# A planner's durations, landings and fillers: new numbers for the order of a DeltaNet and SwiGLU kernel

## The chip, the cores and the metric

The kernel runs on one core of a Trainium2 chip. A core has TensorE (PE) for matrix products, which go to eight PSUM banks; VectorE (DVE), ScalarE (ACT) and GpSimd (POOL) for elementwise work; and SyncE (SP), which here only issues DMAs. Each engine runs its own instructions in the order in which the program lists them, and waits for the others through semaphores. The metric is the device time of one execution in microseconds. A measured time of this kernel can be told from no change if it differs by over 0.2%.

## The reference

Two blocks follow each other. The first is a delta-rule recurrence, for 4 batches of 8 heads over 768 steps with a head size of 48:

```python
k_n = k / (np.linalg.norm(k, axis=-1, keepdims=True) + 1e-06)
for t in range(S):
    kt, vt, bt = (k_n[:, :, t], v[:, :, t], beta[:, :, t, None])
    y[:, :, t] = np.einsum('bhd,bhde->bhe', q[:, :, t], state)
    v_old = np.einsum('bhde,bhd->bhe', state, kt)
    state = state + bt[:, :, :, None] * np.einsum('bhd,bhe->bhde', kt, vt - v_old)
```

Its output, as 3072 tokens of 384 features, goes through an RMS norm with a gain and a gated FFN of width 1536:

```python
rms = np.sqrt(np.mean(x * x, axis=-1, keepdims=True) + 1e-06)
xn = x / rms * rms_g
g = xn @ w_gate
silu = g * (1.0 / (1.0 + np.exp(-g)))
return (silu * (xn @ w_val) @ w_out).astype(np.float32)
```

The FFN's weights arrive as 64-bit floats.

## The kernel before, in words

**Chunks.** The 768 steps are cut into 12 chunks of 64. Within a chunk the recurrence is solved as a triangular system; from chunk to chunk a state is carried. For each chunk there is a preparation (norms of k, a transpose of k (`turn`, TensorE line 565), the products of k with itself (`scores`, line 588), a solve of small triangular blocks on VectorE, and several round trips through DRAM that put the blocks into other layouts), a part with q (`qpart`), the recurrence proper (`recur`) and the FFN.

**Chunks 0 and 1** are prepared by `prep16`, which solves blocks of 16 steps. The blocks are copied out by ScalarE (L756), written to DRAM (`dm<-at`) and read back as `dg` (`mt<-dm` for chunk 0, `kk<-dm` and `wsum<-dm` for chunk 1). A TensorE step called `coupling` (L778) makes the parts that couple the blocks. In `recur`, a first product (`first_rows`, L1055, for chunk 0; `mr`, L1041, for chunk 1) is followed by three rounds of `couple` (L1067), each with differences on VectorE (`change`, L1112) between; chunk 0 does this for two halves of its heads in turn. Then come the products with q (`pu`, L1077), the new state (`ku`, L1146), the norm, and a transpose (L1217) whose copies (L1221) are the FFN's input `xf`, or `xp1` for chunk 1. The FFN of chunks 0 and 1 (`ffn_plain`, L1284 and L1266) works with the plain weights. Later chunks use `prep`, with blocks of 32, and a form of the FFN with fewer products (`ffn` and `down`, L1377 and L1434) on sums of weights which VectorE makes once (`factors`, L1342; `out_factors`, L1413).

**Weights.** `weights` brings the 64-bit weights in 24 tiles of 768 KB through three raw buffers. ScalarE takes the upper words (L506), VectorE makes a shift, a mask and a product (L494, L497, L502), and then two 32-bit parts are added. For the first `NPE` = 4 tiles TensorE does that addition, as two products with the identity into PSUM (L518, L519), which ScalarE copies out (L523). For the others VectorE adds (L526).

**The planner.** Nothing of the order is written by hand. Every step is given to a planner with its engine, an assumed duration, a priority or due time, what it reads and writes, and the PSUM banks that it takes. `forward` simulates the engines: at each point it takes the step that can start first, and among equals the one with the lower key. `backward` makes new keys from the result, and 60 rounds of this, some with small random shakes, are tried; the order of the round with the earliest simulated end is written out. The assumed numbers thus do not delay anything by themselves on the chip: they set the order in which each engine is given its instructions, and the order of the DMAs on SP's queue.

Three things of it matter here. A DMA has an earliest simulated start (`after`), a transfer time (`work`) and a latency until others may use its data (0.7, for weight tiles 0.7 + 2.0). A TensorE step's duration in the simulation is a number in the code: 0.5 for `coupling`, 0.49 for each half of `first_rows` and `couple`. And up to a simulated time of 70 us, the planned gaps between TensorE's steps are filled with products of the identity with itself (`filler`, L1538), which write a bank that nobody reads. `fillers` decides how many: it takes a planned gap from `a` to `b`, and adds products of four, two or one times 128 columns, until less than 0.3 is left; a gap of over 1.5 is first lengthened by 0.8. Fillers are in TensorE's queue like any other instruction, and a step that comes after them starts after them.

Of the kernel before, what the change touches and what calls it, by code (L numbers as in the profile page):

```python
# [19 lines left out]
W = 32  # L20
L = 16
# [7 lines left out]
STICK = 1.0  # L29
SHAKE = 0.12  # L30


# [20 lines left out]
def fillers(a, b):  # L53

    if a == 0.0:
        return [4, 4, 1]
    n, t = [], a
    while t < b - 0.3:
        n.append(4 if b - t > 1.5 else 2 if b - t > 0.9 else 1)
        t += 0.22 * n[-1] + 0.02  # L60
    return n


class Plan:
# [154 lines left out]
    def run(self, free, filler=None, until=0.0):  # L219
# [19 lines left out]
        for op, s in best[1]:  # L239
# [4 lines left out]
            if filler and op.eng == "PE":  # L244
                if s < until:
                    filler(fillers(pe, s + (0.8 if s - pe > 1.5 and pe else 0.0)))
                pe = s + op.dur
# [9 lines left out]
def kernel(  # L257
# [54 lines left out]

    WLAT = 2.0
    NPE, NRAW, NCV = 4, 3, 2
    WCOL = 768
    CV2 = 90.0
    NK, NKQ = 3, 2
# [69 lines left out]
    def dma(dst, src, prio, r=(), w=(), work=0.3, dur=0.5, eng="SP", after=0.0):  # L387
        queue = nc.scalar if eng == "ACT" else nc.sync
        op = P.add(eng, dur, lambda: queue.dma_start(out=dst, in_=src), prio, r, w, lat=0.7)  # L389
        op.dma, op.work, op.ready, op.port = True, work, after, False  # L390

    PERIOD = 51.0
# [53 lines left out]
    def zeros_out():  # L446
        dma(dm.rearrange("g x s t -> (g x s t)").rearrange("(p n) -> p n", n=1024), mt[0].rearrange("p x t -> p (x t)"),
            5, r=mtkeys(0), w=[("dm", z) for z in range(4)], work=2.0, dur=0.6, after=16.8)

    def load_small():  # L450
        for i in range(8):
            src = beta.rearrange("b (y g) (c i t) -> i g (b y) c t", i=2, g=2, t=W)[i // 2 % 2, i % 2]
            dma(beta_b[16 * i : 16 * i + 16], src, 0.5, w=[("beta", i)], work=0.2, after=0)
        for z in range(2):
            rows = slice(64 * z, 64 * z + 64)
            P.add("ACT", 0.25, lambda rows=rows, z=z: nc.scalar.copy(b16[rows], beta_b[rows, 0:2, L * z : L * z + L]), 3, r=[("beta", i) for i in range(4 * z, 4 * z + 4)], w=[("b16", z)])
        dma(g_sb, moe_rms_g.rearrange("(t p) -> p t", p=128), 1, w=["g"], after=33)

# [5 lines left out]
    def weights():  # L464
# [14 lines left out]
        for n, (dst, src, keys) in enumerate(todo):  # L479
# [3 lines left out]
            rdst = raw[i].rearrange("p (a c) -> p a c", a=parts)  # L483
            dma(rdst, src, (0.1 if n == 0 else 3 + 2 * n), w=[("raw", i)], dur=0.7, work=3.06, after=(6.0, 29.5, 32.8, 33.1, 41.3, 40.8, 44)[n] if n < 7 else 48)

            P.ops[-1].lat = 0.7 + WLAT
            low, high = (raw[i].bitcast(U32)[:, w_ : w_ + 2 * WCOL - 1 : 2] for w_ in range(2))
# [45 lines left out]
    def load(c, what):  # L533
        t0 = c * C
        pk, pq, pv = ((-5, 1, 12), (5, 29, 36))[c] if c < 2 else (due(c, 150), due(c, 99), due(c, 70))
        if "q" in what and c > 1:
            for d, eh, g, th in itertools.product(range(2), repeat=4):
                e0, e1 = 32 * eh, min(D, 32 * eh + 32)
                src = q.rearrange("b (yh a) t e -> a t (b yh) e", a=4)[2 * d + g, t0 + 32 * th : t0 + 32 * th + 32, :, e0:e1]
                r0 = 64 * d + 32 * eh  # L540
                dma(q2t[r0 : r0 + 32, :, g, th, 0 : e1 - e0], src, pq, w=[q2k[8 * d + 4 * eh + 2 * g + th]], work=0.2, after=40.1)
        for key, t, src, pr in (("k2", k2[c % NK], k, pk), ("q2", q2, q, pq)):
            for g in range(2):
# [3 lines left out]
                s = src.rearrange("b (y g) t e -> g t (b y) e", g=2)[g, t0 : t0 + C]  # L547
                dma(dst, s, pr, w=[(key, c % NK, g)] if key == "k2" else q2k[8 * g : 8 * g + 8], dur=0.7, work=1.02, eng="ACT" if c == 0 and g and key == "k2" else "SP", after=((0.0, 18.2, 0.0), (2.9, 46, 0.0))[c]["kqv".index(key[0])] if c < 2 else 40.1)
        if "v" in what and c == 0:
            for g in range(2):  # L550
                s = v.rearrange("b (y g) t e -> g t (b y) e", g=2)[g, 0:C]
                dma(vt[64 * g : 64 * g + 64], s, pv, w=[("v", g)], dur=0.7, work=1.02, after=10.1)
        elif "v" in what:
            for bb in range(2):
                s = v[2 * bb : 2 * bb + 2, :, t0 : t0 + C, :].rearrange("p h t e -> t (p h) e")
                dma(vt[64 * bb : 64 * bb + 64], s, pv, w=[("v", bb)], dur=0.85, work=1.02, after=44.0 if c < 2 else 62.1)

# [78 lines left out]
    def prep16(c):  # L636
# [57 lines left out]
        for r0, b0, n in place:  # L694
            dma(a16[c][r0 : r0 + W], dk.rearrange("g x j t -> (g x) j t")[:, b0 : b0 + L, b0 : b0 + L], pd, r=[("dfull", c, g) for g in range(2)], w=[("ab", c, n)], dur=0.55, work=0.5, after=25 if c else 0.0)
        ab = [("ab", c, n) for n in range(4)]
# [73 lines left out]
        for h in range(2):  # L770
# [10 lines left out]
            P.rows = 64  # L781
            P.add("PE", 0.5, coupling, pi, r=dgk + ["under"] + (kkall if c else []), w=[ps] + ek, ps=ps, size=64)
            P.rows = 128
# [188 lines left out]
    def recur(c):  # L972
# [141 lines left out]
        for h in halves:  # L1114
# [4 lines left out]
            else:  # L1119
                P.add("PE", 0.49, lambda h=h: first_rows(h), pr, r=[("dg", 0, g) for g in range(2)] + mtkeys(0) + vk, w=gu + uk(h) + zk(h), ps=gu, size=64)  # L1120
            P.rows = 128
# [4 lines left out]
            for n in range(3):  # L1126
                P.rows = 64
                P.add("PE", 0.49 * len(h), lambda h=h, t=zb if n else u_: couple(h, t), pr, r=ek + (zk(h) if n else uk(h)), w=gu, size=64 * len(h))
                P.rows = 128
# [444 lines left out]
```

## Time and profile before

| | |
|---|---|
| median of 3 runs | 708.71 us (708.32 to 708.85) |
| the profiled execution | 709.8 us |
| its span, first to last instruction | 708.1 us |
| TensorE busy | 697.1 us (98%) |
| VectorE busy | 538.9 us (76%) |
| ScalarE busy | 305.4 us (43%) |
| fillers (L1538) busy | 43.0 us, all before 72 us |
| granted TensorE clock, mean | 0.999 |

Times in the profile are microseconds from the start of the span. "L778" is line 778 of the kernel. The chain of waits is followed back from the last instruction; each of its rows has a start, a length and what ran. An engine's timeline has start, length, engine, line, operation and tiles, and in brackets how long the engine was idle before and what it waited for. An fp32 product is listed as two instructions, so "x64" is 32 products; a transpose is one. A TensorE that runs fillers counts as busy.

### The profile page before, as it was taken

Reading aid. Unit: us, or ns where it says so; the run is one execution under the profiler, and the core shown is the slowest. Engines: PE = TensorE matmul, PEld = TensorE weight load, DVE = VectorE, ACT = ScalarE, POOL = GpSimd, SP = SyncE. Lnnn points to the kernel's source line nnn. Section 1 sums busy time; section 2 is a strip of 40 time slices with the busy share of each in tenths; the row PEclk is TensorE's granted clock in tenths of the full one; section 3 lists DMA queues with packets and bytes.
Section 4 is the critical chain, followed back from the end, with each engine's and each line's share of the span. In section 5 each row is a group of like instructions: output and inputs, shape, how many; then the busy total and the mean of one; then the engine's idle time right before and its main releaser. Section 6 shows DMA issues by size and latency. Waiting matters only on the chain.

```text
span 708.1 us, 23662 instructions
## 1 busy us (share of the span) xinstructions
PE 697.1 (98%) x10178; PEld 635.7 (90%) x10178; DVE 538.9 (76%) x1129; ACT 305.4 (43%) x739; POOL 141.6 (20%) x143
## 2 busy tenths in 40 slices
PE   9999999999989999999999999999999999999997
PEld 5677887778869999999999989999999999999997
DVE  3553799999999978959849949959869838957473
ACT  5244544343314635544535445445446345236241
POOL 6002012103141332132132132133132103000000
PEclk9999999999999999999999999999999999999999
DMA  7569683664620252353252352343342160030000
GB/s 155 116 183 216 174 215 84 167 119 77 108 53 14 45 104 45 64 94 57 45 96 51 50 90 49 56 82 56 58 88 44 27 116 7 14 65 2 23 1 24
DMA packets 236585, 55.49 MB, mean 78 GB/s; under 512 B 225856, under 2 KB 228928, under 8 KB 236480
## 3 DMA queue, kind: packets, MB, share of 16 engines
q1 hardware_dynamic: 232304, 53.19, 38.6%
q8 instruction: 80, 1.31, 0.8%
q10 hardware_dynamic: 4176, 0.79, 0.5%
q14 instruction: 25, 0.20, 0.1%
HBM read 40.83 MB, written 13.11 MB: 76 GB/s over the span
## 4 chain that ended last, share of the span: by engine, by line
PE 88%; DVE 4%; SPq 3%; DMA 1%; ACT 1%; issue 1%; POOL 0%; ACTq 0%; DVEq 0%; POOLq 0%
PE bank L1377 36%; PE bank L1434 17%; PE bank L1284 7%; PE bank L1538 5%; PE bank L588 4%; SPq L389 3%; PE bank L994 3%; PE bank L1266 3%; PE bank L565 2%; PE bank L1067 2%; PE bank L1077 2%; PE bank L1041 2%; PE bank L1146 1%; DVE w_in L1342 1%; PE bank L1217 1%; PE bank L955 1%
## 5 line engine op out<-in xcount | busy, mean ns | idle before, releaser
L1377 PE MATMUL bank<-xf,w_in 128*128 128x128 f32 x1440 | 180.7, 277 | 0.0
L1377 PEld LDWEIGHTS bank<-xf,w_in 128*128 128x128 f32 x1440 | 170.3, 192 | 2.2 <-issue 0.8
L1387 DVE TENSOR_TENSOR tmp<-tmp,bank 128x512 f32<-128x512 f32 x180 | 120.9, 683 | 63.9 <-PE bank L1377 49.0
L1377 PE MATMUL bank<-xf,more 128*128 128x128 f32 x960 | 124.9, 278 | 2.7 <-DVE tmp L1387 2.7
L1377 PEld LDWEIGHTS bank<-xf,more 128*128 128x128 f32 x960 | 114.9, 192 | 5.2 <-DVE tmp L1387 2.9
L1389 ACT COPY tmp<-bank 128x512 f32<-128x512 f32 x120 | 68.8, 585 | 98.2 <-PE bank L1377 67.9
L1393 ACT ACTIVATE tmp<-tmp 128x256 f32<-128x256 f32 x120 | 49.7, 417 | 84.6 <-DVE tmp L1387 84.2
L886 DVE TENSOR_REDUCE acc<-acc 128x30 f32<-128x90 f32 (+4 forms) x150 | 70.9, 473 | 5.2
L610 POOL TENSOR_TENSOR knrm<-ksum,half 128x16 f32<-128x16 f32 x12 | 35.9, 2994 | 184.0 <-DVE ksum L609 184.0
L1434 PE MATMUL bank<-wo_sb,hf 128*128 128x192 f32 x360 | 63.5, 327 | 0.0
L1434 PEld LDWEIGHTS bank<-wo_sb,hf 128*128 128x128 f32 x360 | 58.1, 190 | 0.1
L1394 DVE TENSOR_TENSOR hf<-tmp 128x256 f32<-128x256 f32 x120 | 50.3, 437 | 6.4 <-ACT tmp L1393 5.9
L880 DVE TENSOR_TENSOR acc<-acc,at 128x60 f32<-128x60 f32 (+4 forms) x150 | 51.4, 343 | 1.7
L1538 PE MATMUL bank<-ident 128*128 128x128 f32 (+2 forms) x154 | 43.0, 425 | 1.4 <-POOL ident masks.py:199 1.4
L906 POOL COPY acc<-acc 128x128 f32<-128x128 f32 x40 | 21.4, 563 | 97.4 <-DVE acc L886 97.0
L1538 PEld LDWEIGHTS bank<-ident 128*128 128x128 f32 x154 | 25.7, 195 | 16.4 <-issue 13.5
L833 POOL TENSOR_TENSOR at<-at,beta_b 128x1024 f32<-128x1024 f32 x8 | 18.9, 2357 | 91.4 <-DMA at<-dkk 56.8
L1266 PE MATMUL bank<-wo_sb,hf 128*128 128x384 f32 x96 | 34.8, 491 | 0.0
L1284 PE MATMUL bank<-xf,w_in 128*128 128x256 f32 x144 | 34.2, 385 | 0.0
L1284 PE MATMUL bank<-xp,w_in 128*128 128x256 f32 x144 | 34.0, 382 | 0.1
L1443 DVE TENSOR_TENSOR tmp<-tmp,bank 128x192 f32<-128x192 f32 x30 | 10.5, 349 | 29.7 <-PE bank L1434 27.9
L1284 PEld LDWEIGHTS bank<-xp,w_in 128*128 128x128 f32 x144 | 26.8, 190 | 5.5 <-ACT xp L1221 0.3
(185 smaller groups left out, 1054.4 us busy)
## 6 DMA issues: line engine op xcount, KB each, us to landing
at<-dkk SPq DMA_DIRECT2D x20, 256.0 KB, 3.8
more<-in_moe_w_gate_dram SPq DMA_DIRECT2D x6, 768.0 KB, 5.3
vt<-in_v_dram SPq DMA_DIRECT2D x24, 192.0 KB, 4.0
more<-in_moe_w_val_dram SPq DMA_DIRECT2D x6, 768.0 KB, 6.8
more<-in_moe_w_out_dram SPq DMA_DIRECT2D x6, 768.0 KB, 4.9
out_dram<-tmp SPq DMA_DIRECT2D x48, 96.0 KB, 2.2
k<-in_k_dram SPq DMA_DIRECT2D x23, 192.0 KB, 4.0
dkk<-kk SPq DMA_DIRECT2D x40, 64.0 KB, 1.9
```

Source lines behind the costliest of these rows:

```text
L610: P.add("POOL", 2.95, lambda: nc.gpsimd.tensor_tensor(out=knrm[i2], in0=ksum[i2], in1=half, op=ALU.pow), pn, r=[("ksum", i2), "half"], w=[ ...
L880: nc.vector.tensor_tensor(out=acc[:, 1:3, 0:n, j + 2 : W].rearrange("p a i t -> p i a t"), in0=acc[:, old, 0:n, j : j + 2, None].to_broadc ...
L886: nc.vector.tensor_reduce(out=acc[:, new, 0:n, j + 2 : W], in_=acc[:, lo : lo + 3, 0:n, j + 2 : W].rearrange("p a i t -> p i t a"), axis=A ...
L1266: nc.tensor.matmul(po[p].t[:, 0:DM], hf[:, spot(f), 128 * p : 128 * p + 128], wo_sb[:, spot(f)], start=(f == f0), stop=(f == f1 - 1), skip ...
L1284: nc.tensor.matmul(ps.t[:, TOK * side : TOK * side + TOK], w_in[:, side, h_, 3 * t + i_, n : n + 128], x_[:, 2 * t : 2 * t + 2].rearrange( ...
L1377: nc.tensor.matmul(g.t[:, 128 * z : 128 * z + 128], fac[:, side, 128 * f : 128 * f + 128], xf[:, xs], start=(begin and z == 0), stop=False ...
L1387: P.add("DVE", V(512), lambda t=t, g=g: nc.vector.tensor_tensor(out=t, in0=t, in1=g.t, op=ALU.add), -1, r=[g], w=[tk], last=g)
L1389: P.add("ACT", A(512), lambda t=t, g=g: nc.scalar.copy(t, g.t), -1, r=[g], w=[tk], last=g)
L1393: P.add("ACT", A(256), lambda t=t: nc.scalar.activation(out=t[:, 0:256], in_=t[:, 0:256], func=ACTF.Silu), -1, w=[tk])
L1394: P.add("DVE", V(256), lambda t=t, f0=f0, p=p: nc.vector.tensor_tensor(out=hf[:, spot(f0) : spot(f0) + 2, 128 * p : 128 * p + 128], in0=t[ ...
L1434: nc.tensor.matmul(g.t[:, 0:192], a_[:, f], b_[:, f], start=(begin and f == 0), stop=(f == 5), skip_group_check=True)
L1538: nc.tensor.matmul(warm[:, 0 : 128 * w_].rearrange("p (w n) -> p w n", n=128), ident, ident[:, None, :].to_broadcast([128, w_, 128]))
```

## The change

All of it is in the numbers that the planner gets, but for one thing: `NPE` becomes 2, so that TensorE adds the parts of the weight tiles 0 and 1 alone, and VectorE those of 2 and 3 as well.

- `fillers` stops when less than 1.0 (`SPARE`) of a planned gap is left, instead of 0.3, and a gap over 1.5 is no longer lengthened.
- `coupling` is planned with 1.04 instead of 0.5, each half of `first_rows` with 1.0 instead of 0.49, and `couple` with 1.14 for a half instead of 0.49.
- The extra latency of 2.0, which only the weight tiles had, is also assumed for q of chunks 0 and 1, for k of chunk 1 and for v of chunk 0.
- The earliest simulated starts of several loads move: beta from 0 to 2.8, the loads of `at` (block reads) for chunk 1 from 25 to 29.5, the first weight tile from 6.0 to 4.7, the fourth from 33.1 to 35.2, the gain vector from 33 to 34.6, the zeroing of `dm` from 16.8 to 16.4, k of chunk 1 from 2.9 to 2.2, k and q of later chunks from 40.1 to 44.5, v of chunk 0 from 10.1 to 10, of chunk 1 from 44.0 to 37.9 and of later ones from 62.1 to 59.7.
- The priority of the weight tiles from the tenth on, `CV2`, goes from 90 to 91.4 (a higher number is later).

```diff
--- before.py
+++ after.py
@@ -28,6 +28,7 @@
 EARLY, FETCH0, AHEAD0 = 130.0, 42.0, 130.0
 STICK = 1.0
 SHAKE = 0.12
+SPARE = 1.0
 
 
 class Op:
@@ -55,7 +56,7 @@
     if a == 0.0:
         return [4, 4, 1]
     n, t = [], a
-    while t < b - 0.3:
+    while t < b - SPARE:
         n.append(4 if b - t > 1.5 else 2 if b - t > 0.9 else 1)
         t += 0.22 * n[-1] + 0.02
     return n
@@ -243,7 +244,7 @@
                     g.t = free.pop(0)[1]
             if filler and op.eng == "PE":
                 if s < until:
-                    filler(fillers(pe, s + (0.8 if s - pe > 1.5 and pe else 0.0)))
+                    filler(fillers(pe, s))
                 pe = s + op.dur
             op.fn()
             for g in op.release:
@@ -310,10 +311,10 @@
 
     more = sbt("more", [128, 6144])
 
-    WLAT = 2.0
-    NPE, NRAW, NCV = 4, 3, 2
+    LATE = 2.0
+    NPE, NRAW, NCV = 2, 3, 2
     WCOL = 768
-    CV2 = 90.0
+    CV2 = 91.4
     NK, NKQ = 3, 2
     k2 = sbt("k2", [128, 16, DP], NK)
     q2 = sbt("q2", [128, 16, DP])
@@ -388,6 +389,7 @@
         queue = nc.scalar if eng == "ACT" else nc.sync
         op = P.add(eng, dur, lambda: queue.dma_start(out=dst, in_=src), prio, r, w, lat=0.7)
         op.dma, op.work, op.ready, op.port = True, work, after, False
+        return op
 
     PERIOD = 51.0
 
@@ -445,16 +447,16 @@
 
     def zeros_out():
         dma(dm.rearrange("g x s t -> (g x s t)").rearrange("(p n) -> p n", n=1024), mt[0].rearrange("p x t -> p (x t)"),
-            5, r=mtkeys(0), w=[("dm", z) for z in range(4)], work=2.0, dur=0.6, after=16.8)
+            5, r=mtkeys(0), w=[("dm", z) for z in range(4)], work=2.0, dur=0.6, after=16.4)
 
     def load_small():
         for i in range(8):
             src = beta.rearrange("b (y g) (c i t) -> i g (b y) c t", i=2, g=2, t=W)[i // 2 % 2, i % 2]
-            dma(beta_b[16 * i : 16 * i + 16], src, 0.5, w=[("beta", i)], work=0.2, after=0)
+            dma(beta_b[16 * i : 16 * i + 16], src, 0.5, w=[("beta", i)], work=0.2, after=2.8)
         for z in range(2):
             rows = slice(64 * z, 64 * z + 64)
             P.add("ACT", 0.25, lambda rows=rows, z=z: nc.scalar.copy(b16[rows], beta_b[rows, 0:2, L * z : L * z + L]), 3, r=[("beta", i) for i in range(4 * z, 4 * z + 4)], w=[("b16", z)])
-        dma(g_sb, moe_rms_g.rearrange("(t p) -> p t", p=128), 1, w=["g"], after=33)
+        dma(g_sb, moe_rms_g.rearrange("(t p) -> p t", p=128), 1, w=["g"], after=34.6)
 
     def spot(f):
 
@@ -481,9 +483,9 @@
             i, a = n % NRAW, n % NCV
             parts = dst.shape[1]
             rdst = raw[i].rearrange("p (a c) -> p a c", a=parts)
-            dma(rdst, src, (0.1 if n == 0 else 3 + 2 * n), w=[("raw", i)], dur=0.7, work=3.06, after=(6.0, 29.5, 32.8, 33.1, 41.3, 40.8, 44)[n] if n < 7 else 48)
-
-            P.ops[-1].lat = 0.7 + WLAT
+            dma(rdst, src, (0.1 if n == 0 else 3 + 2 * n), w=[("raw", i)], dur=0.7, work=3.06, after=(4.7, 29.5, 32.8, 35.2, 41.3, 40.8, 44)[n] if n < 7 else 48)
+
+            P.ops[-1].lat = 0.7 + LATE
             low, high = (raw[i].bitcast(U32)[:, w_ : w_ + 2 * WCOL - 1 : 2] for w_ in range(2))
             top, cc = cva[a], cvb[a]
             u = top.bitcast(U32)
@@ -538,22 +540,23 @@
                 e0, e1 = 32 * eh, min(D, 32 * eh + 32)
                 src = q.rearrange("b (yh a) t e -> a t (b yh) e", a=4)[2 * d + g, t0 + 32 * th : t0 + 32 * th + 32, :, e0:e1]
                 r0 = 64 * d + 32 * eh
-                dma(q2t[r0 : r0 + 32, :, g, th, 0 : e1 - e0], src, pq, w=[q2k[8 * d + 4 * eh + 2 * g + th]], work=0.2, after=40.1)
+                dma(q2t[r0 : r0 + 32, :, g, th, 0 : e1 - e0], src, pq, w=[q2k[8 * d + 4 * eh + 2 * g + th]], work=0.2, after=44.5)
         for key, t, src, pr in (("k2", k2[c % NK], k, pk), ("q2", q2, q, pq)):
             for g in range(2):
                 if key[0] not in what or key == "q2" and c > 1:
                     continue
                 dst = t[64 * g : 64 * g + 64, :, 0:D]
                 s = src.rearrange("b (y g) t e -> g t (b y) e", g=2)[g, t0 : t0 + C]
-                dma(dst, s, pr, w=[(key, c % NK, g)] if key == "k2" else q2k[8 * g : 8 * g + 8], dur=0.7, work=1.02, eng="ACT" if c == 0 and g and key == "k2" else "SP", after=((0.0, 18.2, 0.0), (2.9, 46, 0.0))[c]["kqv".index(key[0])] if c < 2 else 40.1)
+                op = dma(dst, s, pr, w=[(key, c % NK, g)] if key == "k2" else q2k[8 * g : 8 * g + 8], dur=0.7, work=1.02, eng="ACT" if c == 0 and g and key == "k2" else "SP", after=((0.0, 18.2, 0.0), (2.2, 46, 0.0))[c]["kqv".index(key[0])] if c < 2 else 44.5)
+                op.lat += LATE if c == 1 or key == "q2" else 0.0
         if "v" in what and c == 0:
             for g in range(2):
                 s = v.rearrange("b (y g) t e -> g t (b y) e", g=2)[g, 0:C]
-                dma(vt[64 * g : 64 * g + 64], s, pv, w=[("v", g)], dur=0.7, work=1.02, after=10.1)
+                dma(vt[64 * g : 64 * g + 64], s, pv, w=[("v", g)], dur=0.7, work=1.02, after=10).lat += LATE
         elif "v" in what:
             for bb in range(2):
                 s = v[2 * bb : 2 * bb + 2, :, t0 : t0 + C, :].rearrange("p h t e -> t (p h) e")
-                dma(vt[64 * bb : 64 * bb + 64], s, pv, w=[("v", bb)], dur=0.85, work=1.02, after=44.0 if c < 2 else 62.1)
+                dma(vt[64 * bb : 64 * bb + 64], s, pv, w=[("v", bb)], dur=0.85, work=1.02, after=37.9 if c < 2 else 59.7)
 
     def turn(src, dst, keys, r, pr, split):
 
@@ -692,7 +695,7 @@
         turns = itertools.cycle(("SP",) if c else ("SP", "ACT"))
         place = [(64 * z + W * i, W * i + L * z, 2 * z + i) for z in range(2) for i in range(2)]
         for r0, b0, n in place:
-            dma(a16[c][r0 : r0 + W], dk.rearrange("g x j t -> (g x) j t")[:, b0 : b0 + L, b0 : b0 + L], pd, r=[("dfull", c, g) for g in range(2)], w=[("ab", c, n)], dur=0.55, work=0.5, after=25 if c else 0.0)
+            dma(a16[c][r0 : r0 + W], dk.rearrange("g x j t -> (g x) j t")[:, b0 : b0 + L, b0 : b0 + L], pd, r=[("dfull", c, g) for g in range(2)], w=[("ab", c, n)], dur=0.55, work=0.5, after=29.5 if c else 0.0)
         ab = [("ab", c, n) for n in range(4)]
         ak = [("acc", c)]
         bkeys = [("b16", 0), ("b16", 1)]
@@ -779,7 +782,7 @@
 
             ek = [("ET", h, bb) for bb in range(2)]
             P.rows = 64
-            P.add("PE", 0.5, coupling, pi, r=dgk + ["under"] + (kkall if c else []), w=[ps] + ek, ps=ps, size=64)
+            P.add("PE", 1.04, coupling, pi, r=dgk + ["under"] + (kkall if c else []), w=[ps] + ek, ps=ps, size=64)
             P.rows = 128
             for bb in range(2):
                 dst = et[:, 8 * bb + 4 * h : 8 * bb + 4 * h + 4]
@@ -1117,7 +1120,7 @@
             if c:
                 P.add("PE", 0.49 * len(h), lambda h=h: mr(h), pr, r=mtk + rhsk, w=gu + uk(h), ps=gu, size=64 * len(h))
             else:
-                P.add("PE", 0.49, lambda h=h: first_rows(h), pr, r=[("dg", 0, g) for g in range(2)] + mtkeys(0) + vk, w=gu + uk(h) + zk(h), ps=gu, size=64)
+                P.add("PE", 1.0, lambda h=h: first_rows(h), pr, r=[("dg", 0, g) for g in range(2)] + mtkeys(0) + vk, w=gu + uk(h) + zk(h), ps=gu, size=64)
             P.rows = 128
             evacuate(h, c > 1)
             if c > 1:
@@ -1125,7 +1128,7 @@
             ek = [("ET", p, bb) for p in h for bb in range(2)]
             for n in range(3):
                 P.rows = 64
-                P.add("PE", 0.49 * len(h), lambda h=h, t=zb if n else u_: couple(h, t), pr, r=ek + (zk(h) if n else uk(h)), w=gu, size=64 * len(h))
+                P.add("PE", 1.14 * len(h), lambda h=h, t=zb if n else u_: couple(h, t), pr, r=ek + (zk(h) if n else uk(h)), w=gu, size=64 * len(h))
                 P.rows = 128
                 if n < 2:
                     change(h)
```

## The prediction

> **What bounds the kernel now.** I read the page first, then the windows, the chain in order of time, and last the timelines of ScalarE, VectorE and the DMA for the first 72 us. The page's head:
>
> ```profile
> span 708.1 us, 23662 instructions
> PE 697.1 (98%) x10178; PEld 635.7 (90%) x10178; DVE 538.9 (76%) x1129; ACT 305.4 (43%) x739; POOL 141.6 (20%) x143
> ```
>
> TensorE seems full from end to end. But part of that is dummy products: line 1538 is the filler. The chain of waits from 24 us to 72 us (start, length, what):
>
> ```profile
> 25.06 3.02 PE bank L1538 x12
> 28.08 0.87 PE bank L565 x8
> 28.95 3.02 PE bank L1538 x10
> 31.98 1.09 PE bank L588 x64
> 33.07 6.22 PE bank L1538 x18
> 39.29 2.01 PE bank L778 x64
> ...
> 46.69 1.06 PE bank L1067 x32
> 47.76 2.36 PE bank L1538 x8
> 50.12 1.06 PE bank L1067 x32
> 51.18 0.64 PE bank L1538 x4
> ...
> 62.27 3.00 PE bank L1538 x10
> 65.26 0.66 PE bank L1217 x6
> ```
>
> The chain goes through fillers: the real work behind a filler started when the filler ended, not when its data came. The L1538 rows of the chain after the first add up to 37.2 us before 72 us. Two looks show that data was there earlier. ScalarE and VectorE, timeline:
>
> ```profile
> 26.25 0.27 DVE L745 TENSOR_REDUCE acc<-acc 128x28 f32<-128x84 f32 x1
> 28.55 0.59 ACT L577 COPY qt<-bank 128x512 f32<-128x512 f32 x1 [3.09 <-PE bank L565]
> 29.04 0.52 ACT L756 COPY at<-acc 128x128 f32<-128x128 f32 x2
> 32.57 0.62 ACTq L389 DMA_DIRECT2D mt<-dm x1
> ```
>
> The block solve of chunk 0 ends at 26.52 on VectorE. Its next step, the copy L756, stands in ScalarE's queue behind the q copy L577, which waits for a transpose (L565) that waits for a filler. Then the reload mt<-dm, issued at 32.57, lands after 3.9 us by the issue table, at 36.5, and L778, which needs it, starts at 39.29 behind 6.22 us of filler. Windows (the columns are busy time by engine, granted clock, DMA share and GB/s):
>
> ```profile
> 65.10:72.00 6.90, 6.90 (x88) 4.50 (x86) 2.57 (x5) 5.62 (x14) 1.88 (x2) 1.00 0.95 154
> 90.00:185.00 95.00, 94.85 (x1385) 74.35 (x1384) 90.26 (x176) 36.32 (x81) 17.43 (x16) 1.00 0.57 128
> 65.10:209.30 144.20, 142.07 (x1900) 111.81 (x1898) 129.66 (x234) 57.48 (x130) 27.35 (x23) 1.00 0.59 128
> ```
>
> So three stages: to 65 us fillers and delay; from 65 to 209 us TensorE nearly full with real work and VectorE (third count) 95% busy from 90 us; after that TensorE alone, with 2.2 us of idle time between 212 and 660 us in the windows.
>
> **The change part by part.** The profiled execution took 709.8 us: its span of 708.1 and 1.7 around it. The median is 708.71, 1.1 less. Gains are taken from the first and applied to both alike.
>
> *Shorter fillers, longer planned steps.* A filler is cut where the planned gap is under 1.0 (before 0.3), and a gap over 1.5 is no longer lengthened by 0.8. The coupling steps were planned at half their length: 0.49 in the code, 1.06 in L1067's rows, so the plan saw gaps that TensorE did not have. With 1.14, what follows a half's step until its next one is 0.2 + two differences of 0.34 + 0.15, 1.0 us, and the other half's 1.14 covers it: no gap is planned there, and no filler. Four places on the path:
>
> (a) The first scores, L588, start at 9.71; their last input, VectorE's copy of kt (7.76, 0.68 long), is ready at 8.44. Late by 1.2. The store dfull and the loads of at follow it, so it passes on. Bounds 0 and 1.2; I take 1.0.
>
> (b) L756 could start at 26.6 and starts at 29.04: 2.5 late. q is now assumed to land 2.0 later, which puts its transpose and copy behind L756 in the order. If the order stays, the filler is 1.5 shorter but its end 2.0 later: 0.5 lost. Bounds -0.5 and 2.5; I take 2.3, because the plan orders by readiness.
>
> (c) L778: 39.2 against 36.5, 2.7 late. Bounds 0 and 2.7; I take 2.2, with some planned gap left.
>
> (d) From 39.29 to 65.26, 25.97 us hold 13.3 us of filler rows. Needed waits inside are the last half's evacuation, some 0.45, and the scaling of yn: L1077 ends at 60.3 and yn is done at 62.7, 2.4, of which the 0.86 of L1146 is useful. So 11.3 could go. VectorE also does parts of two weight tiles here (2.06 each: 0.55, 0.56, 0.95), which were covered by fillers and may now show: I take 8.0. Bounds 0 and 11.3.
>
> Together 13.5 us at L1217, with bounds -0.5 and 17.7.
>
> *Two weight tiles added on VectorE instead of TensorE.* Tiles 2 and 3 cost TensorE 0.86 + 0.86 + 0.43 + 0.43 each, at 68.50 and 73.65, so 5.2 us leave TensorE's full stretch; ScalarE loses four copies (1.9 us); VectorE gets two additions of 0.95 (row L526), 1.9 us. TensorE waits 2.73 us at 207.3 for VectorE, so VectorE already trails by that: of 5.2 I count 2.5. Bounds -1.9 (VectorE decides alone) and 5.2.
>
> *What is late next.* An earlier L1217 wants chunk 1's blocks earlier too. They are issued from 54.4 to 64.2 and the last lands at 69.2 (5.0 after issue); L778 uses them at 76.2. With everything 16 us earlier it would be 60.2. From 44 to 72 us the DMA share in steps of 4 us is 0.17, 0.61, 0.66, 1.22, 1.14, 0.97, 0.94: 6.6 us of idle time in all, so they land at 62.6 at best. The other products of chunk 0's FFN fill part of it. Cost 0 to 9; I take 4.
>
> *Moved loads.* SP issues in order. beta (five issues of 2.80 us ahead of k of chunk 1) goes behind k: eight issues of 0.55 from about 3, landing 3.1 later, by 11; bk needs it at 14.85, so nothing, unless beta lands after that; but ScalarE's copies of beta (L456) stand ahead of L653 at 10.97, on path (a), and if the order keeps them there it starts 0.3 later, inside what (a) leaves. The first weight tile (7.76 to about 6.5) gets an earlier conversion; VectorE starts it at 16.41 when other work allows: nothing. The zeroing of dm stands behind the loads of at and lands long before dm's blocks: nothing. v of chunk 1 may go earlier, but waits for L1055 to have read vt; what stands behind it on SP waited 7.8 us for L756, until 45.3, anyway. k and q of chunk 2, now from 44.5, were issued at 48.8 and later: nothing, nor the gains vector (used at 65.6) and tile 3 (used at 68.4). The loads of at for chunk 1, from 29.5, were issued at 30.54: 0 to 1 on chunk 1's chain, inside the 4. POOL's steps (L610, L672) keep their inputs; k of chunk 1 a little earlier does no harm. The later priority of tiles 9 to 23 changes the order only; if one comes late its consumer's product waits, bounded by the conversion's 3.0 us.
>
> *After 209 us* the work is the same; the planner's search starts from other numbers and gives another order. Idle now 2.2 us; I take no change, bounds 2.2 less and, as below, 13.6 more.
>
> Sum: 13.5 + 2.5 - 4.0 = 12.0 us. 709.8 - 12 = 697.8 for a run like the profiled one, 696.7 by the median: 697.
>
> **Rivals.** *VectorE holds the second stage.* From 65.1 to 209.3 it works 129.7 of 144.2 us. If the weight conversions keep their times, only its longest idle stretch goes, 7.0 us before 69.36 (ScalarE's L506, queued behind the late xf copies), less the 1.9 added: 5.1, so 703.6. For it: 95% from 90 us. Against: at 95%, 131.6 us need 138.5, less than the 144.2 it has, so it can follow an earlier start.
>
> *The data is late, not TensorE.* Then idle time takes the fillers' place, and only the 2.5 of the two tiles is won: 706.2. For it: no row of TensorE shows a wait that could prove the contrary. Against: 26.52 against 29.04, and 36.5 against 39.29.
>
> *TensorE slows down without fillers; slower than before.* The first three fillers, from 1.41, took 4.21 us; two of 512 columns at 0.86 (L518) and one of 128 at a quarter of it make 1.94. So an idle TensorE starts at half speed. The real work from 9.78 to 72 us is 27.6 us; at half speed all of it costs 27.6, and the result is 724; if only L778 to L1217 (12.7 us) is slow, 709.4. It turns against the change from 12 us of slowed work on. Against: after the idle 2.73 us at 207.3, sixteen L1377 took 2.05, as sixteen do elsewhere (1.98), and the planned idle is now 1.0 at most. [...]
>
> *The new order is worse in the ten later chunks.* One chunk now has a wait of 1.5 us for the second merge (423.30, L955 behind ScalarE); nine more make 13.6, and the result is 710.3. Against: nothing in the change touches those steps' durations.
>
> **How the numbers follow.** The forecast, 693 to 702: 0.47. Better, to 686, if chunk 1 follows without loss and VectorE permits: 0.12. VectorE holds: 0.15. Data late: 0.08. Slow TensorE: 0.08. Worse order: 0.08. Others, slower: 0.02. The first four and a little of the next two are faster by more than 0.2% (1.4 us, what a measurement here can tell): 0.83; slower: 0.14; the same: 0.03. The range 689 to 709 leaves out some 0.06 below and 0.14 above; that of the likeliest case alone is 693 to 702.
>
> **What would show it.** Filler rows far below 43.0 us of busy time; L756 straight behind the last L745; L778 within 1 us of the landing of mt<-dm; L1067's six steps within 9 us; L1217 near 52 us; eight matmuls less on each of L518 and L519, two more L526; TensorE's wait for VectorE near 195 us not above 3 us. Wrong if L1217 comes after 60 us, if L1067's steps take 2 us each, or if TensorE stands idle between 55 and 90 us for chunk 1's blocks or weight tiles.

## The result, and the profile after

The changed kernel takes 700.52 us (median of 4 runs, 697.21 to 701.38), the kernel before, run beside it, 708.78. The ratio is 0.9876, with an interval of 0.9842 to 0.991. The prediction was 697.0, faster, within 689 to 709. The run that was profiled took 701.38 us, so all that follows is read from a run at the upper end.

Lines have moved by 2 or 3: L565 is L568 now, L588 L591, L756 L759, L778 L781, L1067 L1070, L1217 L1220, L1284 L1287, L1538 L1541, L518 L520. The head of the page:

```profile
span 699.7 us, 23418 instructions
PE 682.4 (98%) x10066; PEld 621.3 (89%) x10066; DVE 542.1 (77%) x1131; ACT 303.9 (43%) x735; POOL 143.4 (21%) x143
```

TensorE is as full as before, with 14.7 us less of it: 112 matmuls fewer, 96 of them fillers (58 against 154, 25.6 us busy against 43.0) and 16 of the two weight tiles. First the path to the transpose L1220. ScalarE's timeline, then TensorE's (start, length, engine, line, operation, and in brackets the idle time before):

```profile
25.40 0.31 ACT L759 COPY at<-acc 128x128 f32<-128x128 f32 x1 [1.92 <-DVE acc L748]
25.96 0.31 ACT L759 COPY at<-acc 128x128 f32<-128x128 f32 x1 [0.25 <-DVE acc L748]
...
27.26 1.07 ACT L580 COPY qt<-bank 128x512 f32<-128x512 f32 x2 [0.99 <-PE bank L568]
29.30 0.62 ACTq L390 DMA_DIRECT2D mt<-dm  x1
```

```profile
34.18 2.08 PE L781 MATMUL bank<-mt,wsum 64*64 64x64 f32 x64
36.10 2.02 PE L1058 MATMUL bank<-vt,mt 64*64 64x48 f32 x64
38.71 2.07 PE L1070 MATMUL bank<-u,wsum 64*64 64x48 f32 x64 [0.60 <-DVE u L1109]
...
42.08 3.96 PE L1070 MATMUL bank<-state,wsum 64*64 64x48 f32 x123 [0.37 <-issue]
46.03 1.03 PE L1080 MATMUL bank<-u,pt 64*64 64x48 f32 x32
...
51.55 0.49 PE L1220 MATMUL bank<-ident,yn 128*128 128x128 f32 x3
...
55.01 1.56 PE L1287 MATMUL bank<-xf,w_in 128*128 128x256 f32 x6
```

The copies L759 now stand ahead of the q copy and follow the solve (29.04 before). L781 starts at 34.18 (39.22), the six L1070 steps take 38.71 to 46.03 where they took 44.2 to 56.9, and L1220 starts at 51.55 (65.10). Then chunk 1 is not ready. TensorE again, and the windows (busy time by engine, then granted clock, DMA share, GB/s):

```profile
65.30 0.33 PE L781 MATMUL bank<-kk,wsum 64*64 64x64 f32 x2
68.30 1.96 PE L781 MATMUL bank<-kk,wsum 64*64 64x64 f32 x30 [2.67 <-DMA kk<-dm]
70.20 1.97 PE L568 MATMUL bank<-ident,k 128*128 128x128 f32 x8
```

```profile
66.00:68.00 2.00, 0.00 (x0) 0.00 (x0) 1.58 (x3) 0.00 (x0) 0.00 (x0) 0.90 1.16 179
68.00:70.00 2.00, 1.70 (x30) 1.70 (x30) 0.00 (x0) 0.00 (x0) 0.00 (x0) 0.50 0.94 302
70.00:74.00 4.00, 4.00 (x45) 3.43 (x42) 2.16 (x3) 1.54 (x3) 0.00 (x0) 0.50 1.10 348
```

The second block load of chunk 1, kk<-dm, was issued at 62.72 and landed 5.5 us later, at 68.26. TensorE waited 2.67 us for it, and from 67.59 to 74.41 its granted clock was 0.50: eight L568 transposes took 1.97 us instead of 1.04. So the profile shows a gain of 13.5 us at L1220, and a loss that starts 14 us later.

To add this up over a whole run, I use one measure below, the **lost time** by a moment T: T minus the real matmuls finished by T, each row of the trace counted with the time that it takes at full clock (0.43 us for one of 512 columns with the identity, of which a product has two; 0.109 for a transpose; 0.215 for L1284; 0.031 for L778; and so on). Fillers, idle time and slow clock are all in it. That it is good to about 1 us is my estimate; at 660 us it agrees with the difference of the two spans to 0.1 us. Where the two weight tiles are off TensorE, a kernel has 5.2 us less of real work, which comes off besides.

| lost by (us) | 60 | 66 | 76 | 90 | 110 | 212 | 310 | 660 |
|---|---|---|---|---|---|---|---|---|
| before | 40.2 | 44.2 | 44.5 | 44.9 | 45.1 | 50.5 | 52.2 | 61.1 |
| after | 31.3 | 33.3 | 38.6 | 38.8 | 41.6 | 44.3 | 47.3 | 57.9 |

By 660 us 3.2 less is lost; with the 5.2 of work that is 8.4, the difference of the two spans. By 66 us the gain had been 10.9. Between 66 and 76 us 5.3 is lost against 0.3 before (the wait and the half clock), and after 212 us 13.6 against 10.6.

### The profile page after: what moved, and what is told of

Same layout as the page of the kernel before. It is cut to its first block, busy times and chain, and to the rows that moved or that the text cites. A ratio compares the mean times of both kernels' runs of the same rounds, so it can differ in the third digit from the quotient of the medians.

```text
span 699.7 us, 23418 instructions
## 1 busy us (share of the span) xinstructions
PE 682.4 (98%) x10066; PEld 621.3 (89%) x10066; DVE 542.1 (77%) x1131; ACT 303.9 (43%) x735; POOL 143.4 (21%) x143
## 4 chain that ended last, share of the span: by engine, by line
PE 82%; DVE 9%; SPq 3%; DMA 2%; POOL 1%; issue 1%; ACT 1%; DVEq 0%; ACTq 0%; POOLq 0%
PE bank L1380 37%; PE bank L1437 18%; PE bank L1287 7%; PE bank L1269 4%; SPq L390 3%; PE bank L591 3%; PE bank L997 3%; PE bank L568 2%; PE bank L1044 2%; PE bank L1080 2%; PE bank L1541 1%; PE bank L1149 1%; PE bank L1220 1%; PE bank L938 1%; POOL knrm L613 1%
## 5 line engine op out<-in xcount | busy, mean ns | idle before, releaser
L1380 PEld LDWEIGHTS bank<-xf,w_in 128*128 128x128 f32 x1440 | 170.0, 192 | 2.7 <-DVE tmp L1390 0.4
L1390 DVE TENSOR_TENSOR tmp<-tmp,bank 128x512 f32<-128x512 f32 x180 | 120.7, 682 | 52.3 <-PE bank L1380 40.4
L613 POOL TENSOR_TENSOR knrm<-ksum,half 128x16 f32<-128x16 f32 x12 | 35.5, 2959 | 167.5 <-DVE ksum L612 165.9
L883 DVE TENSOR_TENSOR acc<-acc,at 128x60 f32<-128x60 f32 (+4 forms) x150 | 53.9, 359 | 4.4 <-DMA out_dram<-tmp 2.3
L1446 DVE TENSOR_TENSOR tmp<-tmp,bank 128x192 f32<-128x192 f32 x30 | 10.5, 350 | 37.9 <-PE bank L1437 37.9
L909 POOL COPY acc<-acc 128x128 f32<-128x128 f32 x40 | 23.5, 616 | 77.7 <-DVE acc L889 77.5
L1287 PE MATMUL bank<-xf,w_in 128*128 128x256 f32 x144 | 34.8, 388 | 0.1
L1287 PE MATMUL bank<-xp,w_in 128*128 128x256 f32 x144 | 33.5, 382 | 0.0
L1287 PEld LDWEIGHTS bank<-xp,w_in 128*128 128x128 f32 x144 | 26.9, 190 | 4.9
L1287 PEld LDWEIGHTS bank<-xf,w_in 128*128 128x128 f32 x144 | 26.3, 190 | 4.7 <-ACT xf L1224 0.5
L1442 ACT COPY tmp<-bank 128x192 f32<-128x192 f32 x30 | 9.7, 322 | 44.0 <-PE bank L1437 42.6
```

Of the source, the lines that this page charges most:

```text
L613: P.add("POOL", 2.95, lambda: nc.gpsimd.tensor_tensor(out=knrm[i2], in0=ksum[i2], in1=half, op=ALU.pow), pn, r=[("ksum", i2), "half"], w=[ ...
L883: nc.vector.tensor_tensor(out=acc[:, 1:3, 0:n, j + 2 : W].rearrange("p a i t -> p i a t"), in0=acc[:, old, 0:n, j : j + 2, None].to_broadc ...
L909: P.add("POOL", 1.2, lambda: spread(xt_, lambda d, t: nc.gpsimd.tensor_copy(out=d, in_=t), True), pi, w=AK)
L1287: nc.tensor.matmul(ps.t[:, TOK * side : TOK * side + TOK], w_in[:, side, h_, 3 * t + i_, n : n + 128], x_[:, 2 * t : 2 * t + 2].rearrange( ...
L1380: nc.tensor.matmul(g.t[:, 128 * z : 128 * z + 128], fac[:, side, 128 * f : 128 * f + 128], xf[:, xs], start=(begin and z == 0), stop=False ...
L1390: P.add("DVE", V(512), lambda t=t, g=g: nc.vector.tensor_tensor(out=t, in0=t, in1=g.t, op=ALU.add), -1, r=[g], w=[tk], last=g)
```

## The experiments

**Theory.** Fillers stood ahead of work that was ready; the shorter fillers and longer planned steps win the time, and chunk 1's late block takes part of it back. **Rivals**: the assumed landings do it; the two weight tiles do it; or any other order of the planner would. Each kernel is compared with the kernel before on the same chip: 709.89 us for `e1` to `e4`, 709.16 for `e5` to `e8`, 709.88 for `e9` to `e12`.

**The parts alone.** `e1` has the new fillers only, `e2` the new durations only, `e3` both, on the kernel before with its landings and its four TensorE-summed tiles.

```diff
-    while t < b - 0.3:
+    while t < b - 1.0:
-                    filler(fillers(pe, s + (0.8 if s - pe > 1.5 and pe else 0.0)))
+                    filler(fillers(pe, s))
```

```diff
-            P.add("PE", 0.5, coupling, ...
+            P.add("PE", 1.04, coupling, ...
-                P.add("PE", 0.49, lambda h=h: first_rows(h), ...
+                P.add("PE", 1.0, lambda h=h: first_rows(h), ...
-                P.add("PE", 0.49 * len(h), lambda h=h, t=zb if n else u_: couple(h, t), ...
+                P.add("PE", 1.14 * len(h), lambda h=h, t=zb if n else u_: couple(h, t), ...
```

> The kernel before with the shorter fillers alone (gap limit 1.0, no lengthening by 0.8). Theory A (fillers stood ahead of ready work in chunk 0): the transposes L1217 start near 57 us instead of 65.1, and the time falls by about 5 us, to 704. Rival B (the two weight tiles taken off TensorE made the gain): within 1.5 us of before. Rival C (a luckier order made the gain): any value, with L1217 hardly moved.

> The kernel before with the longer planned coupling steps alone (1.04, 1.0, 1.14). Theory A: the fillers inside the six L1067 steps go, those before L588, L565 and L778 stay; L1217 near 60 us, the time near 705. Rival B: within 1.5 us of before.

> The kernel before with shorter fillers and longer planned steps together, old landings and four tiles on TensorE. Theory A: L1217 near 54 us and 701 to 704, most of the gain of the whole change. Rival B: 706 or more, because the 5.2 us of the two tiles are still on TensorE.

Measured: `e1` 702.43 us, ratio 0.9897 [0.985, 0.9945]; `e2` 703.52, 0.9917 [0.9889, 0.9945]; `e3` 699.31, 0.9857 [0.9827, 0.9887]. The fillers' busy time is 28.3, 34.5 and 23.7 us, and the first L1217 starts at 60.17, 60.16 and 58.15. In `e1` and `e3` L778 now waits for its data, in two pieces, as the waits of `e3` show:

```profile
PE bank L778 <- DMA mt<-dm: 1.8, 2, 0.9
```

Either edit alone wins 6 to 7.5 us, both together 10.6 us, by the ratio no less than the whole change, although L1217 comes 6.6 us later than in the changed kernel. What `e3` wins by 66 us it keeps, as the table below shows: it loses 35.6 by 66 and 36.2 by 90.

**The landings alone.** The changed kernel with old fillers, old durations and four tiles:

```diff
-SPARE = 1.0
+SPARE = 0.3
-                    filler(fillers(pe, s))
+                    filler(fillers(pe, s + (0.8 if s - pe > 1.5 and pe else 0.0)))
-    NPE, NRAW, NCV = 2, 3, 2
+    NPE, NRAW, NCV = 4, 3, 2
```

and 0.5, 0.49 and 0.49 for the planned steps.

> The changed kernel with the fillers, the planned durations and the four TensorE-summed tiles of before: only the landings, the earliest starts and CV2 are new. Theory A: the gain comes from the fillers and the durations; the landings alone put the copy L759 ahead of the q copy (2.3 us of the prediction) and nothing else, and the fillers behind still hold most of that: 706 to 710. L1220 not before 61 us, fillers above 38 us of busy time. Theory B: the landings are a gain of their own, by which the plan follows the chip: L1220 before 59 us and 702 or less.

Measured: 710.75 us, ratio 1.0018 [0.9993, 1.0042]. L759 is ahead of the q copy, at 26.57, and still nothing is won. TensorE's timeline of `e10` shows where the 2.5 us went:

```profile
34.94 5.86 PE L1541 MATMUL bank<-ident 128*128 128x512 f32 x16
40.73 2.08 PE L781 MATMUL bank<-mt,wsum 64*64 64x64 f32 x64
```

The data of L781, mt<-dm, landed at 35.83; L781 stands behind a filler of 5.86 us and starts later than before (39.22). So the landings alone are worth nothing, as the theory had it. Beside the new fillers they may be worth something, which the next two groups show.

**The two weight tiles.** `e4` is the changed kernel with `NPE = 4`; `e9` the kernel before with `NPE = 2`.

> The changed kernel with four weight tiles added on TensorE again. Theory A: 0 to 2.5 us slower than the changed kernel, 700.5 to 703, since TensorE stood idle 3.3 us between 60 and 72 us anyway. Rival B: 5 us slower, 705 to 706.

> The kernel before with NPE = 2 alone, so that VectorE adds the parts of the weight tiles 2 and 3; fillers, planned durations and landings as before. Theory A: the step with the tiles is worth what the prediction said wherever TensorE has other work ready, and the kernel before has it from 65 to 90 us: 5.2 us of its work go, VectorE gets 1.9 more, so 704.6 to 707 beside 709.2 for before. It cost time in the changed kernel only because there TensorE ran out of other work at 65 us. Theory B: the two tiles' sums are needed as cover in any case: 709 to 714, with TensorE idle between 65 and 80 us. Another order in the later chunks can move either by some 2 us, so the sum of TensorE's idle time up to 90 us decides before the end does.

Measured: `e4` 693.08 us, ratio 0.9762 [0.9747, 0.9778], the fastest of all kernels here, where both expectations were above 700; `e9` 711.74, 1.003 [1.001, 1.0049]. Taking work off TensorE made both slower. In `e4` the sums of the two tiles stand at 55.07 to 57.65 and 60.11 to 62.80, and what comes after them is (TensorE's timeline):

```profile
67.59 0.33 PE L781 MATMUL bank<-kk,wsum 64*64 64x64 f32 x2
68.72 1.91 PE L781 MATMUL bank<-kk,wsum 64*64 64x64 f32 x58 [0.81 <-DMA kk<-dm]
...
73.98 2.07 PE L1070 MATMUL bank<-u,wsum 64*64 64x48 f32 x64
```

The block lands at the same time, but TensorE reaches it 2.3 us later, waits 0.81 us, keeps its clock (1.00 granted from 64 to 76 us; 58 matmuls in 1.91 us), and starts L1070 at 73.98 instead of 77.48 with 5.2 us more work done. In `e9` fillers took the place of the freed time (TensorE's timeline):

```profile
80.53 2.43 PE L1538 MATMUL bank<-ident 128*128 128x512 f32 x8
82.89 2.07 PE L1067 MATMUL bank<-u,wsum 64*64 64x48 f32 x64
84.89 2.86 PE L1538 MATMUL bank<-ident 128*128 128x512 f32 x10
```

These 5.3 us did not exist before, where all fillers ended before 72 us. So without these sums the plan has gaps at 80 and 85 us, and fills them. That TensorE had no other work there does not follow. The first of the two fillers stands ahead of L1067, whose inputs were written by 78.9 us; the last of them on VectorE's timeline:

```profile
78.40 0.42 DVE L790 COPY wsum<-bank 128x256 f32<-128x256 f32 x1
```

So at least 2.4 us of what `e9` loses is again a filler ahead of ready work, and theory A is off in its time, but `e9` does not refute its reason, that TensorE has other work ready there.

**Another order.** The planner's random shakes with seed 48 instead of 47: `e6` for the changed kernel, `e7` with `NPE = 4` besides, `e8` for the kernel before.

```diff
-random.Random(47)
+random.Random(48)
```

> The changed kernel with another seed for the planner's shakes: the same assumptions, another order. Theory A2: L1220 again near 52 us, and the time between 693 and 702, by what becomes of the wait before chunk 1's coupling and of the later chunks. Rival C (the gain of the change is a lucky order): 705 or more.

> The changed kernel with four tiles on TensorE and the other seed. Theory A2 (the two tiles' 5.2 us on TensorE stand where it would wait for chunk 1's blocks, and keep its clock): faster than the same seed with two tiles, by 2 to 7 us. Rival C (the 7 us between two and four tiles are the order's luck): no faster than with two tiles, or slower.

> The kernel before with the other seed. Theory A2: the same fillers and short planned steps, so L1217 at 63 to 67 us, and 706 to 711. Rival C: a spread as large as the gain, 700 or less.

Measured: `e6` 700.31 us, 0.9861 [0.9835, 0.9887]; `e7` 700.1, 0.9854 [0.9825, 0.9883]; `e8` 709.89, 1.0003 [0.9987, 1.0018]. The change's gain holds with this other order, and this other order alone gives none. But the 7.4 us between `e4` and the changed kernel (8.1 by the ratios) do not hold: with seed 48 it is 0.2. The wait before L781 came again in `e6`, 3.13 us long, and in `e7` it was 0.97 us. The lost times tell what of it belongs to the tiles:

| lost by (us) | 60 | 66 | 76 | 90 | 110 | 212 | 310 | 660 |
|---|---|---|---|---|---|---|---|---|
| `e3`, fillers and durations | 35.5 | 35.6 | 36.1 | 36.2 | 37.4 | 40.0 | 42.6 | 50.6 |
| `e4`, after with 4 tiles | 31.0 | 31.3 | 32.4 | 32.7 | 33.5 | 35.8 | 38.2 | 44.4 |
| `e6`, after, seed 48 | 31.0 | 33.8 | 40.5 | 40.5 | 41.9 | 44.8 | 49.4 | 56.8 |
| `e7`, 4 tiles, seed 48 | 31.8 | 31.9 | 33.7 | 34.9 | 35.8 | 38.6 | 43.5 | 51.5 |
| `e9`, before with 2 tiles | 40.4 | 44.2 | 45.0 | 50.9 | 51.3 | 55.8 | 57.7 | 67.4 |
| `e11`, after, k later | 32.1 | 32.5 | 32.8 | 33.2 | 42.2 | 48.1 | 50.4 | 62.4 |
| `e12`, `e11` with 4 tiles | 30.8 | 30.9 | 31.3 | 32.1 | 39.5 | 47.4 | 49.3 | 59.3 |

By 76 us the kernels with two tiles have lost 6.2 us more (after against `e4`) and 6.8 more (`e6` against `e7`), by 90 us 6.0 (`e9` against before). The work saved is 5.2. So in all three pairs the step itself costs 0.8 to 1.6 us by then, in two of them through the wait and in `e9` through fillers. The rest of the 7.4 lies in the later chunks: from 90 to 660 us after loses 19.1 and `e4` 11.7, but `e6` 16.3 and `e7` 16.6.

The table also shows what the landings do beside the new fillers. `e4` differs from `e3` by the landings and `CV2` alone. It takes 6.2 us less, its L1220 starts at 51.83 where L1217 of `e3` starts at 58.15, and by 90 us it has lost 3.5 us less. That is one order; `e7`, with another, takes as long as `e3`.

**Fillers against the half clock.** If the slow clock is the dear part of the wait, fillers in the gap should win it back. `e5` puts fillers of 512, 512, 512 and 256 columns in front of chunk 1's `coupling`.

```diff
+            op.hold = [4, 4, 4, 2] if c and not h else []
...
+                filler(op.hold)
             op.fn()
```

> The changed kernel with 3.0 us of fillers (14 times 128 columns) put ahead of the coupling step of chunk 1, where TensorE stood idle for 2.7 us and then ran at a granted clock of 0.50. Theory A2 (the idle time itself costs little, the slow clock after it some 4 us): granted clock 1.00 between 68 and 74 us, the lost time there 3 to 4 us smaller, 696 to 698 in every run, with a mean clock of 0.999. Rival D (the wait for the blocks sets the pace and the slow clock is hidden behind it): within 1.5 us of the changed kernel's 700.5.

Measured: 699.74 us, 0.9845 [0.981, 0.9881], with runs from 696.6 to 701.07, so not 696 to 698 in every run, and by the time alone not told apart from rival D. Here all lines are two or three further on. In the profiled run the idle time came earlier, in three waits for wsum<-dm of 0.46, 0.56 and 0.95 us, and the clock fell before the fillers were reached (windows of `e5`, columns as above):

```profile
64.00:68.00 4.00, 3.89 (x64) 3.35 (x65) 3.42 (x7) 1.41 (x2) 0.00 (x0) 0.59 1.35 194
```

The coupling behind the fillers ran at full clock, 32 matmuls in 1.15 us, but started at 71.29. The next step, L1073, started at 77.77, as late as in the changed kernel (77.48). Whether a filler at the right place would save the 3 us is left open.

**The block earlier.** In the changed kernel SP issued q and two loads of k for chunk 2 between 60.2 and 62.7 us, ahead of kk<-dm. `e11` assumes these loads later; `e12` does so with four tiles.

```diff
-... if c < 2 else 44.5)
+... if c < 2 else 66.0)
-... pq, w=[q2k[8 * d + 4 * eh + 2 * g + th]], work=0.2, after=44.5)
+... pq, w=[q2k[8 * d + 4 * eh + 2 * g + th]], work=0.2, after=66.0)
```

> The changed kernel with the earliest simulated start of k of chunk 2 and later, and of q of chunk 2 and later, at 66 instead of 44.5: SP then issues the second kk<-dm straight behind the four wsum<-dm, ahead of q and of the two loads of k that stood before it from 60.2 to 62.7 us. Theory A: these loads made the block late, and the wait for it together with the half clock after it cost 5 us. Then kk<-dm lands by 66 us, L781 of chunk 1 waits under 1.0 us for it, the granted clock stays above 0.9 in every 4 us from 60 to 90, L1070 of chunk 1 starts by 75 us (77.5 in the changed kernel), and the time is 694 to 697, with the runs within 2 us of each other. Theory B: the DMA engines are full from 48 to 72 us, so the block lands near 68 us in any order: the wait stays at 2 to 3 us, 699 to 702. A start by 75 us with a time above 699 would say that the later order gives the gain back.

> The same with four TensorE-summed tiles (5.2 us more work for TensorE). Theory A: with the block there in time, TensorE has work anyway, and two more tiles cost what they take: 3 to 5 us more than the kernel with two, so 697 to 701. Theory B: the two tiles help by themselves, and the 693.1 of the changed kernel with four tiles comes back or is beaten: 690 to 694. Between the two, 694 to 697, the order of the later chunks decides and nothing is told apart.

Measured: `e11` 704.41 us, 0.9928 [0.9903, 0.9952]; `e12` 707.84, 0.9988 [0.9961, 1.0016]. Both are slower than either theory expected. The first half of theory A held, and theory B, by which the block lands near 68 us in any order, did not. SP's and TensorE's timelines of `e11`:

```profile
58.99 0.63 SPq L390 DMA_DIRECT2D kk<-dm  x1
```

```profile
62.29 2.28 PE L781 MATMUL bank<-kk,wsum 64*64 64x64 f32 x60
...
94.53 2.41 PE L1070 MATMUL bank<-r,wsum 64*64 64x48 f32 x64 [0.67 <-DVE r L1115]
98.97 1.15 PE L1080 MATMUL bank<-u,pt 64*64 64x48 f32 x64 [2.03 <-DVE u L1109]
...
105.57 0.48 PE L591 MATMUL bank<-qt,kt 64*64 64x64 f32 x5 [3.80 <-issue]
```

The block is there 6 us earlier, L781 waits 0.2 us at most, the clock stays at 1.00 in every window to 90 us, and by 90 us only 33.2 us are lost, 5.6 less than after. The second half fell. L1070 came at 86.44 instead of 77.48, with FFN products ahead of it in the order. Between 90 and 110 us TensorE ran dry, with waits of 0.67, 2.03 and 3.80 us, and the clock fell to 0.50 once more (windows of `e11`):

```profile
102.00:106.00 4.00, 0.43 (x9) 0.35 (x9) 3.90 (x9) 2.56 (x6) 3.31 (x3) 0.81 1.12 254
106.00:110.00 4.00, 4.00 (x88) 3.42 (x90) 3.90 (x7) 2.09 (x6) 2.14 (x2) 0.50 0.84 218
```

Between 90 and 110 us `e11` loses 9.0 us where the changed kernel loses 2.8, so at 110 us the gain of 5.6 is gone (42.2 against 41.6). VectorE (third count) is full in these windows; what the wait of 3.80 us was for, the trace does not show. `e11` and `e12` show one thing more: by 90 us the difference of lost time is only 1.1, so with the block in time the two tiles off TensorE are worth 5.2 - 1.1 = 4.1 us, and the times differ by 3.4.

## Why the prediction was right, point by point

- **(a), first scores, 1.0 taken**: L591 at 7.86 instead of 9.71, 1.85, and its end is 1.64 earlier. That is above the bound of 1.2: VectorE's copy of kt ends at 8.47, as before, but the first of these products need only the other part of kt, and the step had counted from the last input. **(b), 2.3 taken**: mt<-dm issued at 29.30 instead of 32.57, 3.27 earlier, of which 1.85 is (a): 1.4. **(c), 2.2 taken**: L781 5.04 earlier, so 1.8. The whole lateness of 2.7 is gone, since L781's weight loads wait 0.76 us for the data; but the load took 4.8 us instead of 3.9. **(d), 8.0 taken**: 13.55 less 5.04, 8.5. Together 13.5, as predicted; the parts missed by up to 0.9 each way, so that the sum is exact is luck. That fillers held the work back is shown by `e1` to `e3`: fillers and durations alone bring 7.0 of the 13.5. The other 6.6 came only with the landings beside them; with the old fillers (`e10`) the earlier copy won nothing.
- **Two weight tiles, 2.5 taken (-1.9 to 5.2)**: the step that failed in its reason. By 76 to 90 us it measured -0.8 to -1.6 in three pairs and 4.1 in the fourth. I had taken VectorE as what limits the gain, because of its wait at 207 us. VectorE was 92.0 of 95 us busy between 90 and 185 us and TensorE's waits there (1.4 us) were for ScalarE. What decided in the changed kernel was that the 5.2 us stood where TensorE soon after had nothing to do: "TensorE's full stretch" was full with work that could have been done at any time. With seed 48 it was the same; with the block in time (`e11`, `e12`) it was not.
- **Late next, 4 taken (0 to 9)**: right in its place, chunk 1's block, and only in part in its cause. The prediction let the blocks come 16 us earlier and held them back by the full DMA engines alone (share 1.0 or above in the windows 48 to 56 and 64 to 68), to 62.6 at best. In fact the first store of chunk 1's blocks was issued at 43.23 instead of 45.29 and the last reload at 62.72 instead of 64.22; it landed at 68.26 where it had landed at 68.60. The order of SP's queue is the larger part of the last step: in `e11` the reload was issued 3.7 us earlier and its data was used from 62.29, 6.0 us earlier. The loss from L1220 to 90 us was 13.5 less the 6.1 that the table leaves, 7.4, of which 5.0 came between 66 and 76 us; 6.2 of it went with the tiles in `e4`. This term and the one before are not two independent ones: their sum was taken as -1.5 and measured 5.2 - 7.4 = -2.2.
- **No change after 209 us (2.2 less to 13.6 more)**: by 90 us the changed kernel is 6.1 + 5.2 = 11.3 us ahead, where the sum said 12.0. The rest of the miss, 2.9 us, came after 90 us: 2.6 between 100 and 110 us and 3.0 after 212 us, against 2.7 won between 110 and 212 us, where the wait of 2.73 us for VectorE is gone. Kernels whose later steps are untouched lose 11.7 to 19.8 us from 90 to 660 us. The zero was one draw from a spread of 8 us; the range of the likeliest case, 693 to 702, needed some 4 us to each side for this term alone.
- **The rivals.** "VectorE holds the second stage": no; between 90 and 212 us TensorE has no wait for VectorE. "The data is late": no for chunk 0, where L1220 came 13.5 us earlier; yes for chunk 1. "TensorE slows down without fillers": in part; 67.59 to 74.41 us ran at half clock and cost some 3 us (half of 68.30 to 74.41), not the 12 that turn the sign. The profiled runs of `e1` and `e3` had a mean clock of 0.995 and 0.998, and still won: 704.92 and 699.67 us. "Worse order": 3 us instead of 13.6.
- **What would show it.** Fillers 25.6 us; L759 straight behind L748; L781 straight behind the landing of its data; L1070's steps within 7.3 us; L1220 at 51.55; eight matmuls fewer on L520 and L521 each; two more additions: all as said. Of the signs for "wrong", TensorE's idle time between 55 and 90 us for chunk 1's blocks came. But it is not the whole of the miss against 697: by 90 us the changed kernel was ahead by 0.7 us less than the sum said, and 2.9 us were lost after that.

## What to carry to other kernels

Before work is taken off an engine that looks full, ask whether that work stands in front of a wait: if it does, it is cover, and taking it away may win nothing until the wait is gone too. Here 5.2 us of work off TensorE cost 0.2 and 7.4 us with the wait in place, and won 3.4 us with the wait gone. Dummy work in an in-order queue should be counted as delay for whatever stands behind it: in `e10` the data landed at 35.83, and its user started at 40.73, behind the filler. So compare the end of the producer with the start of the consumer, not the engine's busy share. Where an edit reaches the schedule through a search, run it with a second seed before a difference of one per cent is put down to the edit.

## What the runs showed of the hardware that I had not expected

The clock fell to half in or right after idle times of under 3 us, and not each time. In the changed kernel it fell at 67.59, inside the idle time of 2.67 us. In `e10` it fell near 253.2 us, after 2.58 us of idle time (windows):

```profile
252.00:254.00 2.00, 0.65 (x12) 0.49 (x16) 2.00 (x5) 0.00 (x0) 0.00 (x0) 0.80 0.00 0
254.00:256.00 2.00, 2.00 (x61) 1.91 (x58) 2.00 (x4) 0.00 (x0) 0.00 (x0) 0.50 0.03 8
```

In `e5` it fell behind three waits of 0.46, 0.56 and 0.95 us within 3 us: 1.00 from 60 to 64 us, 0.59 from 64 to 68. In the kernel before, 2.73 us idle at 207.3 us left it at 1.00 in every window from 200 to 216 us. So the length of one idle time does not tell these cases apart; what does is left open.

The half clock lasted 6.83 us in the changed kernel. From the granted clocks of the windows I estimate 6.8 us in `e10` (0.80 from 252 to 254, 0.50 from 254 to 260, 1.00 from 260 on), 3.4 in `e5` (0.59 from 64 to 68, 0.98 from 68 to 72) and 10.2 in `e11` (0.81 from 102 to 106, 0.50 from 106 to 114, 0.91 from 114 to 118).

Runs of one kernel differ in their mean clock: for the changed kernel it is 0.995 in the two of 701.3 and 701.4 us, 0.998 at 699.7, 0.999 at 697.2; for `e1` it is 0.999 and 1.000 in the two below 700 us, 0.995 and 0.993 at 704.9 and 706.7. That the spread comes from the half clock is argued from this order, not shown.
